# Other DMA rings for gates, rows and v tiles, and a new engine order, at the start of an attention and feed-forward kernel

## Chip, cores, metric

One core of one Trainium2 chip. The metric is device microseconds of one execution; lower is better. Times are medians of the executions of one kernel. Engines: PE is TensorE (PEld its weight loads), ACT is ScalarE, DVE is VectorE, POOL is GpSimd, SP is SyncE, which here only issues DMA; a "q" behind a name (SPq, ACTq, POOLq) marks its DMA issues. Every execution has a mean granted TensorE clock beside its time, 1.00 being full speed.

## The reference

```python
# q, k, v: (8 batches, 8 heads, 576, 64); f: (8, 8, 576) in 0.8 .. 1.0
scores = matmul(q, k^T) / 8
cum    = cumsum(log(clip(f, 1e-4, 1)), axis=-1)
scores = where(causal, -1e9, scores + cum[..., :, None] - cum[..., None, :])
x      = softmax(scores) @ v                  # heads put side by side: 4608 tokens x 512
out    = (silu(x @ w_gate) * (x @ w_val)) @ w_out     # 512 -> 1536 -> 512
```

## The kernel before

Everything runs in bf16 on PE. The decay enters the scores as extra rows of the operands: four bf16 rows (8 cum, and -8 cum in three parts `hi`, `mid`, `lo`) are computed on 64 partitions and put by DMA under q and k, on partitions 64 to 67 of `QK`. So no score can start before its rows have landed. The second half of a sequence needs the second half of the rows.

A planner in Python gives every operation an engine, the operations it waits for, a priority (`key`) and an earliest time (`ready`), simulates the engines, and emits the instructions in the order so found.

The parts that matter here:

```python
def ld_f(e, c):                     # gates, two halves of a sequence
    E[e].dma_start(out=lf[:, CUTS[c]], in_=f.rearrange("b h s -> (b h) s")[:, CUTS[c]])
o_f   = [op(("ACT", 0.5), ld_f, c, key=-20, ...) for c in range(2)]
o_dec = [op(("DVE", 0.25), fill, dec[r][:, 0 if r else 1], 1.0, key=-17) for r in range(4)]
# ... clip, Ln, scan, hi, mid, lo of each half ...

def row(e, r, c):                   # one decay row (4 in a set) into QK, on SyncE
    E[e].dma_start(out=QK[D + r : D + r + 1, p0:p1, :, x]..., in_=dec[r][2 * p0 : 2 * p1, :, x])

def blank(e, what):                 # GpSimd memsets of QK's tails, of VB's pads ...
    nc.gpsimd.memset(QK[:, :, 1::2, S:], 0.0) ...

def ld_v(e, b, n, bv):              # v tile n of batch b: 128 rows (the last: 64) x 8 heads, float32
    m = min(P, S - n * P)
    nc.sync.dma_start(out=natv[bv.i][:m], in_=v[b, :, n * P : n * P + m].rearrange("h p d -> p h d"))

def cast_v(e, b, n, bv):            # to bf16, for batch 0 on GpSimd
    copy(e, VB[hvb[b].i][:m, n, :, :D], natv[bv.i][:m])

def mask(e, h, i):                  # causal mask of the exponentials, on GpSimd
    nc.gpsimd.affine_select(out=d, in_=d, ...)

W_AT = [-2.8, -18.4, -0.5, 15.6]; CHAIN = 30.6; KEY_Q = -17.9      # (cut: priorities that a search tuned)
V0_KEY = (-1.0, -3.2, 17.1, 22.4, 21.2)                            # v tiles 0..4 of batch 0
```

The first batch goes through attention in two parts: its first 256 queries (`PTa`) and the rest (`PT`, called the second part below). For each part: scores on PE, exponentials on ScalarE, masks on GpSimd, products with v on PE. The weights `wg` and `wv` of the feed-forward stream in meanwhile on GpSimd's DMA queue, with a conversion to bf16.

The softmax here doesn't subtract the row's maximum and nothing guards it: scores larger than these inputs give would overflow.

Of the kernel before, what the change touches and what calls it, by code (L numbers as in the profile page):

```python
# [9 lines left out]
F32 = mybir.dt.float32  # L10
BF16 = mybir.dt.bfloat16
AF = mybir.ActivationFunctionType
ALU = mybir.AluOpType
# [20 lines left out]
class Plan:  # L34
# [32 lines left out]
    def run(self, idle=None):  # L67
# [6 lines left out]
        busy = {e: 0.0 for e in engines}  # L74
        ready = {e: [] for e in engines}
        lanes = [0.0] * 8
        rings, moved = {"HW": [], "POOL": []}, 0.0
        nlane, left, t, seq = 0, len(self.ops), 0.0, 0
        events = []

        def share(busy):
            if rings["POOL"] and rings["POOL"][0][1] is None:
                return [1.0 if r is rings["POOL"] else 0.1 for r in busy]
            return [0.6, 0.65] if len(busy) > 1 else [1.0]

        def push(at, kind, o):
            nonlocal seq
# [6 lines left out]
        while left:  # L94
# [4 lines left out]
            while events and events[0][0] <= t + 1e-9:  # L99
                _, _, kind, o = heapq.heappop(events)  # L100
                if kind in ("queue", "dma"):
                    busy_rings = [r for r in rings.values() if r]
                    for r, x in zip(busy_rings, share(busy_rings)):
                        r[0][0] -= (t - moved) * x
                        while r and r[0][0] < 1e-6:
                            over, n = r.pop(0)
                            if r:
                                r[0][0] += over
                            if n is None:
                                continue  # L110
                            n.done = t + 1.0
                            push(n.done, "end", n)
                            push(n.done + n.late, "done", (n, None, False))
                    moved = t
                    if kind == "queue":
                        r = rings["POOL" if o.ran == "POOL" else "HW"]
                        if o.ran == "POOL" and not r:
                            r.append([1.5, None])
                        r.append([o.dma, o])
                    busy_rings = [r for r in rings.values() if r]  # L120
                    if busy_rings:
                        push(t + min(r[0][0] / x for r, x in zip(busy_rings, share(busy_rings))), "dma", None)
                elif kind == "ready":
                    for e in o.eng:
                        ready[e].append(o)
                elif kind == "end":
                    if o.dma is not None and o.lane is not None:
                        lanes[o.lane] = t
                    for b in o.use:
                        b.left -= 1  # L130
                        if not b.left:
                            self.free[b.pool].append(b.i)
                    left -= 1
                elif kind == "done":
                    o, e, own = o
                    for s in o.next:
                        if (list(s.eng) == [e]) != own:
                            continue
                        s.wait -= 1
                        if not s.wait:  # L140
                            push(max(t, s.ready), "ready", s)
# [61 lines left out]
def kernel(ctx, tc, q, k, v, f, w_gate, w_val, w_out, out):  # L203
# [5 lines left out]
    P = 128  # L209
# [113 lines left out]

    def scan(e, c):
        x = CUTS[c]
        nc.vector.tensor_tensor_scan(out=cum[:, x], data0=lf[:, x], data1=zero[:, x], op0=ALU.add, op1=ALU.add,
                                     initial=cum[:, HALF - 1 : HALF] if c else 0.0)

    def scaled(e, dst, src, x):
# [11 lines left out]
    def fill(e, dst, x):  # L341
        E[e].memset(dst, x)

    o_f = [op(("ACT", 0.5), ld_f, c, key=-20, dma=(0.3, 0.35)[c]) for c in range(2)]
    o_one = op(("DVE", 0.1), fill, warm, 1.0, key=-20)
    o_wln = op(("ACT", 1.5), lambda e: nc.scalar.activation(warm, warm, AF.Ln), after=[o_one], key=-18)
    o_id = op(("POOL", 0.8), lambda e: make_identity(nc, ident[:, :]), key=KEY_Q + 3.5)
    o_zero = op(("DVE", 0.55), fill, zero, 0.0, key=-18)
    o_dec = [op(("DVE", 0.25), fill, dec[r][:, 0 if r else 1], 1.0, key=-17) for r in range(4)]
    ROWS0 = ((0, FB, CUTS[0]), (0, FB, CUTS[1]), (FB, FIRST * FB, slice(0, S)))  # L350

    def row(e, r, c):
# [7 lines left out]
    for c in range(2):  # L360
        x, kc, d = CUTS[c], (-50, CHAIN)[c], (256, 320)[c] / 960
        o = op(("DVE", 0.15 + d), clip, c, after=[o_f[c]], key=-51)
        o = op(("ACT", 0.2 + d), log, c, after=[o, o_wln], key=-51)
        o_ln = o
        o_cum = op(("DVE", 0.15 + 1.9 * d), scan, c, after=[o, o_zero, o_cum], key=kc)
        o_hi = op(("DVE", 0.2 + 0.6 * d), scaled, dec[1][:, 1, x], cum[:, x], -8.0, after=[o_cum], key=kc)
        o_up = op({"ACT": 0.2 + d, "POOL": 0.3 + d}, scaled, dec[0][:, 0, x], cum[:, x], 8.0, after=[o_cum], key=kc)
        o_r1 = op(("DVE", 0.15 + d), rest, x, after=[o_hi], key=kc)
        o_mid = op(("DVE", 0.15 + 0.6 * d), scaled, dec[2][:, 1, x], r1[:, x], 1.0, after=[o_r1], key=kc)
        o_lo = op(("DVE", 0.15 + d), lowest, x, after=[o_mid], key=kc)  # L370
        o_chain += [o_up, o_hi, o_mid, o_lo]
        for n in ((0,), (1, 2))[c]:
            o_row.append([op((ROWQ[c], 0.75), row, r, n, after=[o_dec[r]] + o_chain[r::4], key=ROW_KEY[n] + r, dma=(0.1, 0.1, 0.2)[n],
                             ready=(0, 0, ROW_AT)[n] + 0.8 * r) for r in range(4)])

    def blank(e, what):
# [8 lines left out]
        else:  # L385
            nc.gpsimd.memset(VB[what][:, :, :, D:], 1.0)
            nc.gpsimd.memset(VB[what][LAST:, NB - 1], 0.0)

    o_vb = [op(("POOL", 0.8), blank, 0, key=-15), op(("POOL", 0.8), blank, 1, key=2020, ready=24.0),
            op(("POOL", 0.8), blank, 2, key=4020, ready=40.0)]  # L390
    o_qkz = op(("POOL", 0.9), blank, "qk", key=-14)
    o_pt = op(("POOL", 1.4), blank, "pt", key=310, ready=10.0)
    o_edge = op(("SP", SPi), blank, "edge", after=[o_qkz], key=900, dma=0.2, ready=30)
    o_warm = op(("ACT", 1.4), lambda e: nc.scalar.activation(warm, lf[:1, :1], AF.Exp), after=[o_ln], key=-51)
# [45 lines left out]

    def ld_v(e, b, n, bv):
        m = min(P, S - n * P)
        nc.sync.dma_start(out=natv[bv.i][:m], in_=v[b, :, n * P : n * P + m].rearrange("h p d -> p h d"))

    def cast_v(e, b, n, bv):
        m = min(P, S - n * P)
# [4 lines left out]

    def values(b, n, key, after=(), ready=0.0):
        bv = Buf("nv")
        o = op(("SP", SPi), ld_v, b, n, bv, take=[bv], key=key, dma=1.2 if n < NB - 1 else 0.6, after=after,
               ready=ready, late=LATE if b >= FIRST else LATE0, tag=("ldv", b, n))
        eng = copier(H * D, False) if b == 1 else ("POOL", pool(H * D))
        v_ready[b, n] = op(
            eng, cast_v, b, n, bv, after=[o, o_vb[b % NVB]], use=[bv], key=key, tag=("castv", b, n),
            **({"take": [hvb[b]]} if n == 0 else {}),
        )  # L460
        if n:
            v_ready[b, n].use.append(hvb[b])
            hvb[b].left += 1
            v_ready[b, n].after.append(v_ready[b, 0])
# [5 lines left out]
    def queries(p, key, after=(), ready=0.0):  # L470
        done = []
        b = p // FB
        if b < PEB:
            rest = []
            for x, nm in enumerate("qk"):
                bn, bt = Buf("natw" if b == 1 else "nat"), Buf("t", ("f", BORROW), ("s", 22.0))
                kk = key + 2 * x
                o1 = op(("POOL", 0.35), ld_qk, p, nm, bn, take=[bn], key=kk, dma=0.74,
                        ready=max(ready, release(p) - SLACK) + 0.3 * x, tag=("ldqk", p), late=(0.0, LATE0, LATE)[b])
                o3 = op(("PE", mm(*[QP] * QT)), turn, bn, bt, after=[o1, o_id], take=[bt], use=[bn], key=kk, tag=("turn", p))  # L480
                if b == 1:
                    wo_free.append(o3)
                for a in range(2):
                    first = not rest and not a
                    rest.append(op(
                        {"ACT": 0.75, "DVE": 0.8}, straighten, p, x, a, bt, after=[o3] + ([rest[0]] if rest else []),
                        take=[hqk[p]] if first else [], use=[bt] if first else [bt, hqk[p]], key=kk, tag=("str", p),
                    ))
# [275 lines left out]
    return plan, span  # L764


W_AT = [-2.8, -18.4, -0.5, 15.6]
WO_AT = [28.1, 28.3, 50.7, 57.5]
Q1_AT = [24.1, 27.1, 27.5, 39.5]
V1_AT = 28.1  # L770
CHAIN = 30.6
DEC_AT = 38.0
V0_KEY = (-1.0, -3.2, 17.1, 22.4, 21.2)
V0_AT = (4.8, 3.2, 1.8, 10.5, 7.7)
NARROW_AT = 72.0
FREE = 87.7
LATE = 2.0
ROWS = ("SP", 0.45)
SLACK = 24.0
IDLE_TO = 40.0  # L780
BORROW = 33.9
KEY_Q = -17.9
ROWQ = ("SP", "SP")
ROW_KEY = (-17.7, 22.4, 64.6)
ROW_AT = 28.1
LATE0 = 1.0
# [1 line left out]
_INS = ['q', 'k', 'v', 'f', 'moe_w_gate', 'moe_w_val', 'moe_w_out']  # L788
_OUTS = [((4608, 512), 'float32')]
# [25 lines left out]
```

## Time and profile before

| | value |
|---|---|
| time, median of 3 | 407.28 us (406.62 to 407.53) |
| profile: span, PE busy, mean granted clock | 404.9 us, 96%, 0.978 |
| first score / first exponential of the second part | 14.52 / 27.39 us |
| first product of the second part / first gate matmul | 30.19 / 36.73 us |

From 40 us on PE is full, so only the start is open. The first view is the chain of waits of the kernel before, in order of time (start, length, what; PE, DVE and POOL entries are work, DMA entries transfers, SPq issues):

```profile
1.39 5.33 DMA xT<-in_f_dram
...
13.45 0.38 DVE xT L339
13.83 0.73 SPq L354
...
14.65 10.52 DMA QK<-xT
...
25.31 1.55 PE ps L528 x8
```

The decay arithmetic ends at 13.8 us, its last row is issued at once, and then 10.5 us pass before the rows have landed and PE can score the second part. The timeline of the same stretch (start, length, engine, line, operation, tiles, count; in brackets the idle time before, and its releaser) shows what stands on SyncE's ring between the rows, and what follows:

```profile
10.05 0.73 SPq L443 DMA_DIRECT2D natv<-in_v_dram  x1
10.89 1.50 SPq L354 DMA_DIRECT2D QK<-xT  x2
12.44 0.63 SPq L443 DMA_DIRECT2D natv<-in_v_dram  x1
13.16 2.90 SPq L354 DMA_DIRECT2D QK<-xT  x3
...
25.24 0.61 POOL L302 CAST VB<-natv 128x512 bf16<-128x512 f32 x1 [4.67 <-DMA natv<-in_v_dram]
25.31 1.55 PE L528 MATMUL ps<-QK 68*128 68x192 bf16 x8 [4.51 <-DMA QK<-xT]
27.39 3.73 ACT L536 ACTIVATE PT<-ps 128x512 bf16<-128x512 f32 x9
28.33 0.73 POOL L545 TENSOR_SCALAR_AFFINE_SELECT PT<-PT 128x128 bf16<-128x128 bf16 x3
30.19 0.70 PE L559 MATMUL ps<-VB,PT 128*128 128x65 bf16 x9
```

The DMA queues from 18 to 25 us (packets, MB, share of 16 engines' time):

```profile
q0 software_dynamic: 1314, 0.98, 89.8%
q1 hardware_dynamic: 1314, 0.35, 36.9%
```

q0 is the weights' queue, q1 SyncE's ring: equal counts, but 0.98 MB against 0.35 MB: 1282 of q0's packets have 768 bytes, 1220 of q1's have 256. A v tile of 128 rows x 8 heads is 1024 packets of 256 bytes; the row issued behind it landed at 25.17 us, 10.52 us after its issue.

Last, busy time in stretches of the kernel before (stretch: length, then busy time and count of PE, PEld, DVE, ACT, POOL; then granted clock, DMA share, GB/s):

```profile
11.25:14.66 3.41, 1.73 (x19) 1.18 (x18) 2.54 (x5) 1.83 (x3) 3.41 (x19) 1.00 1.22 181
14.66:18.07 3.41, 3.41 (x32) 2.98 (x31) 1.06 (x2) 2.77 (x5) 1.98 (x4) 0.50 1.28 193
20.00:25.00 5.00, 0.80 (x6) 0.50 (x4) 0.71 (x3) 0.10 (x1) 0.57 (x1) 0.50 1.28 193
25.00:30.00 5.00, 4.69 (x38) 3.60 (x39) 1.56 (x6) 3.37 (x9) 4.38 (x13) 0.50 1.28 195
100.00:200.00 100.00, 99.46 (x828) 55.90 (x826) 60.23 (x113) 58.33 (x121) 35.16 (x99) 1.00 0.77 146
```

PE is busy 0.80 of 5 us from 20 to 25 us and 99.5 of 100 us later. The clock fell to 0.50 at 14.66 us and came back at 31.73 us.

### The profile page before, as it was taken

The page shows a single profiled execution, that of the slowest core. Times are in us where ns is not written, and L with a number is a line of the kernel's source. Part 1 is how long each engine was busy: PE and PEld are TensorE (multiplying, and loading weights), DVE is VectorE, ACT ScalarE, POOL GpSimd, SP SyncE. Part 2 cuts the span into 40 slices and gives each one's busy share as a digit, 9 for nine tenths or more (in the row PEclk, how much of TensorE's full clock was granted, in tenths as well). Part 3 has the DMA queues.
Part 4 walks back from the last instruction along what each step waited for, and adds up shares of the span by engine and source line. Part 5 has one row for each costly group of instructions (what it writes and reads, how often), then busy time and mean ns, then how long its engine had stood idle before and what let it go on. Part 6 is the DMA issues. An engine that isn't in the chain of part 4 may idle for free.

```text
span 404.9 us, 8469 instructions
## 1 busy us (share of the span) xinstructions
PE 388.6 (96%) x3175; PEld 227.3 (56%) x3175; DVE 230.2 (57%) x444; ACT 220.9 (55%) x448; POOL 133.0 (33%) x369
## 2 busy tenths in 40 slices
PE   5859999999999999999999999999999999999996
PEld 4647778645555555555555655655565444444542
DVE  7625888527873477247733775177724861770850
ACT  5738787438764466456465654666666322322321
POOL 8848446803352144225142522542233000000000
PEclk9759999999999999999999999999999999999999
DMA  9999738647944985599579759955211002002002
GB/s 171 189 195 191 168 61 135 94 123 130 155 105 110 174 178 106 126 199 197 116 118 248 131 105 172 192 143 106 52 53 52 2 0 105 1 0 105 0 12 82
DMA packets 103897, 46.57 MB, mean 115 GB/s; under 512 B 87792, under 2 KB 98736, under 8 KB 103536
## 3 DMA queue, kind: packets, MB, share of 16 engines
q1 hardware_dynamic: 92400, 31.72, 37.9%
q0 software_dynamic: 11296, 14.16, 21.8%
q8 instruction: 25, 0.41, 0.4%
q10 hardware_dynamic: 160, 0.15, 0.1%
q14 instruction: 16, 0.13, 0.1%
HBM read 38.34 MB, written 15.78 MB: 134 GB/s over the span
## 4 chain that ended last, share of the span: by engine, by line
PE 85%; DVE 5%; DMA 4%; ACT 1%; issue 1%; POOL 1%; SPq 0%; ACTq 0%; DVEq 0%; POOLq 0%
PE ps L660 42%; PE ps L675 24%; PE ps L528 10%; PE ps L559 7%; DMA QK<-xT 3%; DVE QK L302 2%; PE ps L583 2%; DMA xT<-in_f_dram 1%; DVE hh L671 1%; DVE th L668 1%; POOL wo L410 1%; ACT PT L536 1%; PE ps L416 1%; POOL PT L545 0%; DVE xT L333 0%
## 5 line engine op out<-in xcount | busy, mean ns | idle before, releaser
L660 PE MATMUL ps<-xT,wv 128*128 128x512 bf16 (+3 forms) x480 | 113.0, 357 | 0.0
L660 PE MATMUL ps<-xT,wg 128*128 128x512 bf16 (+3 forms) x480 | 113.0, 357 | 0.0
L668 DVE SCALAR_TENSOR_TENSOR th<-th,ps 128x512 f32<-128x512 f32 (+3 forms) x120 | 75.6, 630 | 55.2 <-ACT th L664 54.9
L675 PE MATMUL ps<-wo,hh 128*128 128x512 bf16 (+1 forms) x444 | 106.5, 379 | 0.0
L664 ACT ACTIVATE th<-ps 128x512 f32<-128x512 f32 (+3 forms) x120 | 66.5, 555 | 69.4 <-PE ps L660 68.1
L536 ACT ACTIVATE PT<-ps 128x512 bf16<-128x512 f32 (+2 forms) x192 | 91.9, 511 | 22.2 <-PE ps L528 13.1
L671 DVE TENSOR_TENSOR hh<-th,ps 128x512 bf16<-128x512 f32 (+3 forms) x120 | 76.1, 635 | 13.2 <-PE ps L660 1.1
L528 PE MATMUL ps<-QK 68*128 68x320 bf16 (+4 forms) x448 | 76.6, 270 | 6.7 <-DMA QK<-xT 5.9
L545 POOL TENSOR_SCALAR_AFFINE_SELECT PT<-PT 128x128 bf16<-128x128 bf16 (+1 forms) x192 | 52.1, 274 | 78.5 <-ACT PT L536 72.5
L660 PEld LDWEIGHTS <-wg 128*128 128x128 bf16 x480 | 44.6, 97 | 36.5 <-issue 0.7
L660 PEld LDWEIGHTS <-wv 128*128 128x128 bf16 x480 | 45.0, 97 | 35.7 <-issue 0.7
L675 PEld LDWEIGHTS <-hh 128*128 128x128 bf16 (+1 forms) x444 | 41.6, 98 | 39.5 <-issue 0.8
L545 POOL TENSOR_SCALAR_AFFINE_SELECT PTa<-PTa 128x256 bf16<-128x256 bf16 x64 | 25.8, 407 | 93.5 <-ACT PTa L536 92.2
L679 ACT ACTIVATE ot<-ps 128x512 f32<-128x512 f32 (+1 forms) x37 | 22.1, 597 | 56.9 <-PE ps L675 56.4
L559 PEld LDWEIGHTS <-PT 128*128 128x128 bf16 x768 | 40.4, 98 | 15.7 <-POOL PT L545 0.4
L559 PE MATMUL ps<-VB,PT 128*128 128x65 bf16 x768 | 48.2, 194 | 0.1
L528 PEld LDWEIGHTS <-QK 68*128 68x128 bf16 x448 | 35.8, 100 | 20.4 <-issue 5.6
L566 DVE RECIPROCAL rc<-ps 128x5 f32<-128x5 f32 (+2 forms) x64 | 12.3, 193 | 54.0 <-PE ps L559 53.8
L536 ACT ACTIVATE PTa<-ps 128x384 bf16<-128x384 f32 x64 | 30.8, 488 | 22.1 <-PE ps L528 22.0
L573 DVE TENSOR_TENSOR xn<-ps,rc 128x320 bf16<-128x320 f32 x56 | 27.5, 492 | 1.9
L302 DVE COPY QK<-ps 64x576 bf16<-64x576 bf16 x24 | 18.7, 797 | 14.1 <-PE ps L416 13.3
L302 DVE COPY xT<-ps 128x576 bf16<-128x576 bf16 (+2 forms) x34 | 14.5, 427 | 20.3 <-PE ps L583 20.3
(47 smaller groups left out, 192.7 us busy)
## 6 DMA issues: line engine op xcount, KB each, us to landing
out_dram<-ot SPq DMA_DIRECT2D x35, 256.0 KB
natv<-in_v_dram SPq DMA_DIRECT2D x32, 256.0 KB
qk_d<-in_q_dram POOLq DMA_DIRECT2D x5, 576.0 KB, 6.9
qk_d<-in_k_dram POOLq DMA_DIRECT2D x5, 576.0 KB, 7.8
wg<-in_moe_w_gate_dram POOLq DMA_DIRECT2D x4, 384.0 KB, 13.4
wv<-in_moe_w_val_dram POOLq DMA_DIRECT2D x4, 384.0 KB, 12.9
wo<-in_moe_w_out_dram POOLq DMA_DIRECT2D x4, 384.0 KB, 5.8
QK<-qk_d SPq DMA_TRANSPOSE x80
```

The costliest lines, as they stand in the source:

```text
L302: E[e].tensor_copy(dst, src)
L528: nc.tensor.matmul(s[:, c : c + w], QK[:KR, hqk[p].i, 2 * j + 1, kt * P : (kt + 1) * P], QK[:KR, hqk[p].i, 2 * j, q0 : q0 + w], start=True ...
L536: nc.scalar.activation(place(h, i)[:, OFFS[i] : OFFS[i] + c], ps(bs)[:, :c], AF.Exp, scale=0.125)
L545: nc.gpsimd.affine_select(out=d, in_=d, pattern=pat, compare_op=ALU.is_ge, fill=0.0, base=0, channel_multiplier=-1,)
L559: nc.tensor.matmul(o[:, lo : lo + D + 1], pt[:, c : c + P], VB[hvb[b].i][:, kt, hb, : D + 1], start=first and n == 0, stop=last and n == l ...
L573: nc.vector.tensor_mul(XN[bx.i][:, qb : qb + nq, j], o, r)
L660: nc.tensor.matmul(ps(bf)[:, :n], w[:, ko, fc * P : (fc + 1) * P], xT[:, ko, t0 : t0 + n], start=(ko == 0), stop=(ko == KD - 1))
L664: nc.scalar.activation(TH[bt.i][:, :n], ps(bf)[:, :n], AF.Tanh, scale=0.5)
L668: nc.vector.scalar_tensor_tensor(out=t, in0=t, scalar=1.0, in1=ps(bf)[:, :n], op0=ALU.add, op1=ALU.mult)
L671: nc.vector.tensor_mul(HH[:, bh.i, lo : lo + n], TH[bt.i][:, :n], ps(bf)[:, :n])
L675: nc.tensor.matmul(ps(bf)[:m, :DM], HH[:, hs[fc].i, lo : lo + m], wo[:, fc, :], start=(fc == 0), stop=(fc == KF - 1))
L679: nc.scalar.activation(OT[bo.i][:m], ps(bf)[:m, :DM], AF.Copy, scale=0.5)
```

## The change

Its intent: let the decay rows land earlier by giving SyncE's ring to gates and rows, and moving the first three v tiles of batch 0 to ScalarE's ring (tile 3 goes early on SyncE, tile 4, of 64 rows, late on SyncE); issue the loads of q and k before GpSimd's memsets; make VectorE's fills shorter by writing two bf16 ones as one float; and let the planner model three rings instead of two, whose shares follow the size of their packets (a model; equal counts of packets, as above, give such shares), with all priorities searched anew.

```diff
-    o_f = [op(("ACT", 0.5), ld_f, c, key=-20, dma=(0.3, 0.35)[c]) for c in range(2)]
+    o_f = [op(("SP", 0.5), ld_f, c, key=-70, dma=(0.3, 0.35)[c], pk=50) for c in range(2)]
...
-    o_zero = op(("DVE", 0.55), fill, zero, 0.0, key=-18)
-    o_dec = [op(("DVE", 0.25), fill, dec[r][:, 0 if r else 1], 1.0, key=-17) for r in range(4)]
+    o_zero = op(("DVE", 0.1), fill, zero[:, :1], 0.0, key=-60)
+    o_dec = [op(("DVE", 0.36), fill, dec[r][:, 0 if r else 1].bitcast(F32), 1.0 + 2.0**-9 - 2.0**-16, key=-52) for r in range(4)]
...
-    o_vb = [op(("POOL", 0.8), blank, 0, key=-15), ...
-    o_qkz = op(("POOL", 0.9), blank, "qk", key=-14)
+    o_vb = [op(("POOL", 0.8), blank, 0, key=KEY_Q + 17), ...
+    o_qkz = op(("POOL", 0.9), blank, "qk", key=KEY_Q + 18)
...
     def ld_v(e, b, n, bv):
-        nc.sync.dma_start(out=natv[bv.i][:m], in_=v[b, :, n * P : n * P + m]...)
+        E[e].dma_start(out=natv[bv.i][:m], in_=v[b, :, n * P : n * P + m]...)
...
-        o = op(("SP", SPi), ld_v, b, n, bv, ...
+        o = op((V0_ENG[n] if b == 0 else "SP", SPi), ld_v, b, n, bv, ..., pk=22, ...
...
-W_AT = [-2.8, -18.4, -0.5, 15.6]
+W_AT = [6.8, -9.5, 10.4, 20.2]
-V0_KEY = (-1.0, -3.2, 17.1, 22.4, 21.2)
-V0_AT = (4.8, 3.2, 1.8, 10.5, 7.7)
+V0_KEY = (-18.9, -18.8, -14.4, 16.0, -20)
+V0_AT = (-0.3, -11.7, 6.9, -18.8, 15.6)
+V0_ENG = ("ACT", "ACT", "ACT", "SP", "SP")
... (cut: the planner's model of the rings; a dozen other priorities)
```

More of the change, by code (lines that the diff above doesn't have):

```diff
@@ L76, in run @@
         lanes = [0.0] * 8
-        rings, moved = {"HW": [], "POOL": []}, 0.0
+        rings, moved = {"SP": [], "ACT": [], "POOL": []}, 0.0
         nlane, left, t, seq = 0, len(self.ops), 0.0, 0
@@ L82, in share @@
             if rings["POOL"] and rings["POOL"][0][1] is None:
-                return [1.0 if r is rings["POOL"] else 0.1 for r in busy]
-            return [0.6, 0.65] if len(busy) > 1 else [1.0]
+                return [1.0 if r is rings["POOL"] else 0.2 for r in busy]
+            x = sum(r[0][1].pk for r in busy)
+            return [(1.15 if len(busy) > 1 and rings["POOL"] else 1.0) * r[0][1].pk / x for r in busy]
         def push(at, kind, o):
@@ L115, in run @@
                     if kind == "queue":
-                        r = rings["POOL" if o.ran == "POOL" else "HW"]
+                        r = rings[o.ran]
                         if o.ran == "POOL" and not r:
@@ L325, in scan @@
         x = CUTS[c]
-        nc.vector.tensor_tensor_scan(out=cum[:, x], data0=lf[:, x], data1=zero[:, x], op0=ALU.add, op1=ALU.add,
+        nc.vector.tensor_tensor_scan(out=cum[:, x], data0=lf[:, x], data1=zero[:, :1].to_broadcast([BH, x.stop - x.start]), op0=ALU.add, op1=ALU.add,
                                      initial=cum[:, HALF - 1 : HALF] if c else 0.0)
@@ L342, in fill @@
         E[e].memset(dst, x)
-    o_f = [op(("ACT", 0.5), ld_f, c, key=-20, dma=(0.3, 0.35)[c]) for c in range(2)]
-    o_one = op(("DVE", 0.1), fill, warm, 1.0, key=-20)
+    o_f = [op(("SP", 0.5), ld_f, c, key=-70, dma=(0.3, 0.35)[c], pk=50) for c in range(2)]
+    o_one = op(("DVE", 0.1), fill, warm, 1.0, key=-61)
     o_wln = op(("ACT", 1.5), lambda e: nc.scalar.activation(warm, warm, AF.Ln), after=[o_one], key=-18)
     o_id = op(("POOL", 0.8), lambda e: make_identity(nc, ident[:, :]), key=KEY_Q + 3.5)
-    o_zero = op(("DVE", 0.55), fill, zero, 0.0, key=-18)
-    o_dec = [op(("DVE", 0.25), fill, dec[r][:, 0 if r else 1], 1.0, key=-17) for r in range(4)]
+    o_zero = op(("DVE", 0.1), fill, zero[:, :1], 0.0, key=-60)
+    o_dec = [op(("DVE", 0.36), fill, dec[r][:, 0 if r else 1].bitcast(F32), 1.0 + 2.0**-9 - 2.0**-16, key=-52) for r in range(4)]
     ROWS0 = ((0, FB, CUTS[0]), (0, FB, CUTS[1]), (FB, FIRST * FB, slice(0, S)))
@@ L372 @@
         for n in ((0,), (1, 2))[c]:
-            o_row.append([op((ROWQ[c], 0.75), row, r, n, after=[o_dec[r]] + o_chain[r::4], key=ROW_KEY[n] + r, dma=(0.1, 0.1, 0.2)[n],
+            o_row.append([op((ROWQ[c], 0.75), row, r, n, after=[o_dec[r]] + o_chain[r::4], key=ROW_KEY[n] + r, dma=(0.1, 0.1, 0.2)[n], pk=34,
                              ready=(0, 0, ROW_AT)[n] + 0.8 * r) for r in range(4)])
@@ L387, in blank @@
             nc.gpsimd.memset(VB[what][LAST:, NB - 1], 0.0)
-    o_vb = [op(("POOL", 0.8), blank, 0, key=-15), op(("POOL", 0.8), blank, 1, key=2020, ready=24.0),
+    o_vb = [op(("POOL", 0.8), blank, 0, key=KEY_Q + 17), op(("POOL", 0.8), blank, 1, key=2020, ready=24.0),
             op(("POOL", 0.8), blank, 2, key=4020, ready=40.0)]
-    o_qkz = op(("POOL", 0.9), blank, "qk", key=-14)
+    o_qkz = op(("POOL", 0.9), blank, "qk", key=KEY_Q + 18)
     o_pt = op(("POOL", 1.4), blank, "pt", key=310, ready=10.0)
@@ L442, in ld_v @@
         m = min(P, S - n * P)
-        nc.sync.dma_start(out=natv[bv.i][:m], in_=v[b, :, n * P : n * P + m].rearrange("h p d -> p h d"))
+        E[e].dma_start(out=natv[bv.i][:m], in_=v[b, :, n * P : n * P + m].rearrange("h p d -> p h d"))
     def cast_v(e, b, n, bv):
@@ L453, in values @@
         bv = Buf("nv")
-        o = op(("SP", SPi), ld_v, b, n, bv, take=[bv], key=key, dma=1.2 if n < NB - 1 else 0.6, after=after,
+        o = op((V0_ENG[n] if b == 0 else "SP", SPi), ld_v, b, n, bv, take=[bv], key=key, dma=1.2 if n < NB - 1 else 0.6, pk=22, after=after,
                ready=ready, late=LATE if b >= FIRST else LATE0, tag=("ldv", b, n))
@@ L477, in queries @@
                 kk = key + 2 * x
-                o1 = op(("POOL", 0.35), ld_qk, p, nm, bn, take=[bn], key=kk, dma=0.74,
+                o1 = op(("POOL", 0.64), ld_qk, p, nm, bn, take=[bn], key=kk, dma=0.74,
                         ready=max(ready, release(p) - SLACK) + 0.3 * x, tag=("ldqk", p), late=(0.0, LATE0, LATE)[b])
@@ L764 @@
     return plan, span
-W_AT = [-2.8, -18.4, -0.5, 15.6]
-WO_AT = [28.1, 28.3, 50.7, 57.5]
-Q1_AT = [24.1, 27.1, 27.5, 39.5]
-V1_AT = 28.1
-CHAIN = 30.6
-DEC_AT = 38.0
-V0_KEY = (-1.0, -3.2, 17.1, 22.4, 21.2)
-V0_AT = (4.8, 3.2, 1.8, 10.5, 7.7)
+W_AT = [6.8, -9.5, 10.4, 20.2]
+WO_AT = [38.8, 38.2, 36.6, 51.1]
+Q1_AT = [19.5, 27.1, 34.3, 41.4]
+V1_AT = 24.4
+CHAIN = 32.3
+DEC_AT = 50.7
+V0_KEY = (-18.9, -18.8, -14.4, 16.0, -20)
+V0_AT = (-0.3, -11.7, 6.9, -18.8, 15.6)
 NARROW_AT = 72.0
-FREE = 87.7
+FREE = 53.2
 LATE = 2.0
@@ L780 @@
 IDLE_TO = 40.0
-BORROW = 33.9
-KEY_Q = -17.9
+BORROW = 34.7
+KEY_Q = -31.3
 ROWQ = ("SP", "SP")
-ROW_KEY = (-17.7, 22.4, 64.6)
-ROW_AT = 28.1
+ROW_KEY = (-20, 13.3, 49.0)
+ROW_AT = -16.2
 LATE0 = 1.0
+V0_ENG = ("ACT", "ACT", "ACT", "SP", "SP")
 _INS = ['q', 'k', 'v', 'f', 'moe_w_gate', 'moe_w_val', 'moe_w_out']
```

## The prediction

The sum came to 4 us: rows landing near 21.5 us for 25.2, exponentials of the second part at 22 to 24 us for 27.4, 403.3 us in total for 407.2. The 270 ns of a shorter fill are the author's estimate, about half of the measured 538. For the dummies, the kernel before shows 0.13 us each at full clock (eight in 1.04 us from 9.60 us) and 0.27 at half (four in 1.06 us from 18.77 us).

> **What bounds it now.** From 40 us on TensorE: the busy times by stretch give PE 99.5 of 100 us from 100 to 200, 100 of 100 from 200 to 300. Only the start is open: the chain of waits reads: the gates' second load (1.39 us, 5.33 us long), decay arithmetic on VectorE among copies of q, k (to 13.8 us), then a 10.5 us wait for the DMA that puts decay rows into QK (14.65 to 25.17); PE resumes at 25.31, ScalarE's exponentials of the second part at 27.4. From 20 to 25 us PE is busy 0.80 of 5 us. The granted clock was 0.50 from about 15 to 31 us.
>
> **Why the rows are late.** In the timeline the rows of the second half are issued at 10.9 to 15.4 us on SyncE, behind two v tiles (10.05, 12.44) of the same ring. From 18 to 25 us the DMA queues moved 1314 packets of GpSimd's weight stream and 1314 of SyncE's: one for one, weight packets of 768 bytes against v packets of 256. So a v tile of 1024 packets crawls, and the rows behind it. [...]
>
> **What changes.**
> - The rows get SyncE's ring with only the gates and one early v tile ahead; three v tiles go to ScalarE's ring. The rows' wait should shrink from 10.5 to about 4.5 us, as for the first rows (issue 9.33 us, scores 14.52).
> - But VectorE's order now clips both halves before the first scan and puts seven copies of q, k (0.8 us each) ahead of the last part of the second half's chain: it ends near 17 us instead of 13.8. Rows land near 21.5 us instead of 25.2.
> - VectorE's five fills of 538 ns become four of about 270 and a tiny one. Worth little: they ended at 4.0 us, when the gates' first half landed (first clip 4.11).
> - GpSimd's memsets (0.74 and 0.95 us) move behind q, k, which are issued up to 1.7 us earlier. Weights start about 2 us later.
> - PE's order holds 73 dummy matmuls for 59; after the first score 29 for 11. At the cold clock they took 0.27 us each: 18 more are 5 us, an estimate. [...] If PE stays warm the dummies are cheap; if cold, they eat the gain.
> - ScalarE's order has all eight first-part exponentials before the second part, which cannot start before about 21 us: the gain is at most about 7 us.
>
> All of this is critical until the second part starts; then PE is full, so the gain should reach the end.
>
> **Prediction.** Second-part exponentials start at 22 to 24 us rather than 27.4; 4 us gained, 403.3 us in total, 8 times in 10 between 399.8 and 407.2. Chances: over 2% faster 0.10, within 2% 0.87, slower 0.03.
>
> **Right if:** the chain shows the rows' wait at 4 to 5 us; PE idle from 20 to 25 us gone; PE from 100 us unchanged, shifted by about 4 us; fills in no wait; first scores within 1 us of 14.
>
> **Wrong if:** the clock stays at 0.50 through 30 us and 29 dummies run at 0.27 us (no gain); the rows still land after 24 us because three rings share the engines; v casts on GpSimd, now behind six weight issues, hold the first products; or later q, k loads of batch 1 delay the first gates (new waits at 35 to 45 us).

## The result, and the profile after

In the first measurement the changed kernel took 405.85 us (median of 404.93, 405.55, 406.15 and one odd execution of 1433.5 us, which the ratio leaves out) against 407.21 us for the kernel before: ratio 0.9961, 95% interval 0.9937 to 0.9984. Measured again, as the first experiment below: 405.14 against 407.49 us, ratio 0.9933 (0.9911 to 0.9955). Ratios are the mean time of one kernel's fast executions over that of the other's in the same rounds, so not quite the ratio of the medians. Between the medians of the fast executions (405.55 us in the first measurement) the gain is 1.7 and 2.4 us, not 4.

The profile of the first measurement fell in the odd execution, in which a 512-column matmul took 820 ns (216 ns in the kernel before, from start to start) while the profile gives the clock as 1.00; it explains nothing about the change. All lines "after" are therefore from the repeat, the same kernel. (Its profiled execution was the slowest of that repeat: 405.95 us, span 404.0 us, clock 0.992.)

The chain of waits of the changed kernel:

```profile
10.34 4.54 DMA QK<-xT
...
18.41 0.68 SPq L356
...
19.14 9.34 DMA natv<-in_v_dram
...
28.53 0.61 POOL VB L303
29.14 0.60 POOL wo L412
29.73 0.32 POOL PT L547
...
30.10 0.46 PE ps L561 x5
```

The rows' long wait is gone from the chain: the first rows cost 4.54 us. In its place stands the last v tile of batch 0: issued on SyncE at 19.14 us, landed 9.34 us later, cast on GpSimd, and only then the first mask and the first product of the second part. The timeline of the changed kernel says the same with the idle times:

```profile
19.14 0.71 SPq L445 DMA_DIRECT2D natv<-in_v_dram  x1
...
23.90 6.12 ACT L538 ACTIVATE PT<-ps 128x512 bf16<-128x512 f32 x15 [2.39 <-PE ps L530]
...
28.53 0.61 POOL L303 CAST VB<-natv 64x512 bf16<-64x512 f32 x1 [3.55 <-DMA natv<-in_v_dram]
29.73 2.82 POOL L547 TENSOR_SCALAR_AFFINE_SELECT PT<-PT 128x128 bf16<-128x128 bf16 x12
30.10 0.46 PE L561 MATMUL ps<-VB,PT 128*128 128x65 bf16 x5 [1.57 <-POOL PT L547]
```

The exponentials of the second part start 3.5 us earlier than before (23.90 for 27.39), as forecast. GpSimd then idles 3.55 us for the tile, with the masks behind it in its list, and the first product starts at 30.10 us, where before it was 30.19. A lead of 3.5 us on ScalarE became one of 0.1 us on PE within six microseconds.

| milestone, us | before | changed (repeat) | lead |
|---|---|---|---|
| first score | 14.52 | 14.97 | -0.4 |
| first exponential of the second part | 27.39 | 23.90 | +3.5 |
| first mask of the second part | 28.33 | 29.73 | -1.4 |
| first product of the second part | 30.19 | 30.10 | +0.1 |
| first gate matmul | 36.73 | 36.13 | +0.6 |
| end of the profile | 404.9 | 404.0 | +0.9 |

The DMA queues of the changed kernel from 19 to 29 us, the time of that tile:

```profile
q0 software_dynamic: 1962, 1.46, 101.1%
q1 hardware_dynamic: 1011, 0.31, 34.3%
```

The tile has 512 packets of 256 bytes. It shared the time with 1962 weight packets, nearly two for each of the 1011 of SyncE's ring. The packet records say more. From 19 to 23 us (`prof again --dma --window 19:23`) SyncE's ring moved 48 packets and the weights' queue 1055; the first 256-byte packet after the tile's issue moved at 23.25 us, 4.1 us after it. So nearly half of the 9.34 us passed before anything of the tile moved; what held it there was not shown, and only in the rest did its packets move beside those of the weights. The kernel before had the same 4.1 us: its 64-row tile, issued at 10.05 us, sent its first packet at 14.17.

Busy time in stretches of the changed kernel:

```profile
20.00:25.00 5.00, 3.74 (x51) 3.22 (x50) 1.79 (x7) 2.61 (x7) 4.98 (x15) 1.00 1.30 199
25.00:30.00 5.00, 3.19 (x22) 1.44 (x20) 1.01 (x5) 5.00 (x13) 1.47 (x4) 0.99 1.41 152
26.45:29.86 3.41, 1.85 (x11) 0.71 (x9) 0.00 (x0) 3.41 (x9) 1.33 (x3) 1.00 1.46 128
29.86:33.27 3.41, 3.17 (x41) 2.69 (x42) 0.58 (x2) 2.40 (x6) 3.41 (x14) 0.50 1.28 193
100.00:200.00 100.00, 99.91 (x841) 56.48 (x840) 60.23 (x114) 59.37 (x121) 35.67 (x101) 1.00 0.80 144
```

PE's gap at 20 to 25 us is filled (3.74 of 5 us for 0.80), at full clock. But from 25 to 30 us PE is busy 3.19 of 5 us, where before it was 4.69. And just when the products come, at 29.86 us, the clock falls to 0.50 until 36.68 us. The stretch 26.45 to 29.86 us, with PE busy 1.85 of 3.41 us, precedes it.

### The profile page after: what moved, and what is told of

Read it like the earlier page. It is cut to its first block, busy times and chain, and to the rows that moved or that the text cites. A ratio compares the mean times of both kernels' runs of the same rounds, so it can differ in the third digit from the quotient of the medians.

```text
span 1431.7 us, 8507 instructions
## 1 busy us (share of the span) xinstructions
PE 1424.2 (99%) x3189; PEld 569.1 (40%) x3189; DVE 233.2 (16%) x447; ACT 237.5 (17%) x444; POOL 135.1 (9%) x370
## 4 chain that ended last, share of the span: by engine, by line
PE 99%; POOL 0%; issue 0%; ACT 0%; ACTq 0%; POOLq 0%
PE ps L662 49%; PE ps L677 25%; PE ps L530 11%; PE ps L561 7%; PE ps L585 2%; PE ps L763 2%; PE ps L418 2%; POOL xT L412 0%; ACT ot L681 0%; POOL ident masks.py:199 0%; POOL ident masks.py:197 0%; ACTq L681 0%; POOLq L802 0%
## 5 line engine op out<-in xcount | busy, mean ns | idle before, releaser
L662 PE MATMUL ps<-xT,wv 128*128 128x512 bf16 (+3 forms) x480 | 388.7, 1020 | 0.0
L662 PE MATMUL ps<-xT,wg 128*128 128x512 bf16 (+3 forms) x480 | 387.7, 1016 | 0.0
L677 PE MATMUL ps<-wo,hh 128*128 128x512 bf16 (+1 forms) x444 | 382.9, 1098 | 0.0
L530 PE MATMUL ps<-QK 68*128 68x320 bf16 (+4 forms) x448 | 210.2, 637 | 0.0
L662 PEld LDWEIGHTS <-wv 128*128 128x128 bf16 x480 | 104.5, 221 | 194.5 <-issue 193.1
L662 PEld LDWEIGHTS <-wg 128*128 128x128 bf16 x480 | 99.8, 212 | 199.1 <-issue 198.3
L677 PEld LDWEIGHTS <-hh 128*128 128x128 bf16 (+1 forms) x444 | 94.1, 216 | 206.4 <-issue 204.9
L561 PEld LDWEIGHTS <-PT 128*128 128x128 bf16 x768 | 106.7, 186 | 77.4 <-issue 65.8
L561 PE MATMUL ps<-VB,PT 128*128 128x65 bf16 x768 | 120.0, 350 | 0.0
L585 PE MATMUL ps<-ident,xn 128*128 128x128 bf16 x160 | 43.2, 493 | 0.0
```

The lines of the kernel that those rows point to most:

```text
L530: nc.tensor.matmul(s[:, c : c + w], QK[:KR, hqk[p].i, 2 * j + 1, kt * P : (kt + 1) * P], QK[:KR, hqk[p].i, 2 * j, q0 : q0 + w], start=True ...
L561: nc.tensor.matmul(o[:, lo : lo + D + 1], pt[:, c : c + P], VB[hvb[b].i][:, kt, hb, : D + 1], start=first and n == 0, stop=last and n == l ...
L585: nc.tensor.transpose(t[:, n * P : (n + 1) * P], XN[bx.i][:, qb + n].rearrange("p h d -> p (h d)"), ident)
L662: nc.tensor.matmul(ps(bf)[:, :n], w[:, ko, fc * P : (fc + 1) * P], xT[:, ko, t0 : t0 + n], start=(ko == 0), stop=(ko == KD - 1))
L677: nc.tensor.matmul(ps(bf)[:m, :DM], HH[:, hs[fc].i, lo : lo + m], wo[:, fc, :], start=(fc == 0), stop=(fc == KF - 1))
```

## The experiments

**Theory A:** the change does what it should for the rows, but GpSimd, waiting for the last v tile, holds the masks and with them the products; a tile that lands early gives back the forecast gain. **Rivals:** B, GpSimd's moved memsets or the order of weights cost the lead; C, the dummy matmuls or the half clock eat it; D, the rows were never worth 4 us.

### again: the changed kernel, once more

No edit.

> The changed kernel unaltered, for a profile of its usual state: its recorded profile fell in an execution of 1433.5 us in which every 512-column matmul took about 820 ns. Expected: 405 to 406 us, ratio to before 0.994 to 0.998. Theory A (the start did gain about 4 us and something after it gave 2.5 us back): second-part exponentials start at 22 to 24 us, and new waits show between 30 and 100 us. Theory B (the start itself gained little): second-part exponentials start at 25 us or later, because rows or v tiles still land late or dummy matmuls fill PE.

Measured: 405.14 us (404.31 to 405.95), 407.49 before, ratio 0.9933 (0.9911 to 0.9955), clocks of the four executions 0.992 to 0.995. The 1433-us execution did not come back, and the gain remains well below 1%.

### v4_act and v4_sp: the last v tile of the changed kernel, issued early

One load moves. In v4_act it follows tile 2 on ScalarE's ring (7.56 us), in v4_sp it follows tile 3 on SyncE's (2.69 us), where 19.14 us was.

```diff
     def ld_v(e, b, n, bv):
+        if (b, n) == (0, NB - 1):
+            return                                    # (cut: an assertion on the buffer)
         E[e].dma_start(out=natv[bv.i][:m], in_=v[b, :, n * P : n * P + m]...)
+        if (b, n) == (0, NB - 2):                     # v4_act: (0, 2)
+            E[e].dma_start(out=natv[NB - 1][:LAST], in_=v[b, :, (NB - 1) * P : S]...)
```

> As v4_act, but issued on SyncE right after its own first v tile (about 2.7 us), before any row. Theory A: the same gain as v4_act, less up to 0.6 us because 512 more small packets run beside the q, k loads and ahead of the first rows. Rival B: no change from the changed kernel, or slower by the 0.6 us.

The 0.6 us in it are the author's estimate; no run measures them alone.

v4_sp measured 403.51 us (402.76 to 403.65) against 407.08, ratio 0.9909 (0.9893 to 0.9925): 3.6 us, the gain that had been forecast for the change. Its timeline:

```profile
25.62 0.64 POOL L303 CAST VB<-natv 64x512 bf16<-64x512 f32 x1
...
26.82 3.11 POOL L552 TENSOR_SCALAR_AFFINE_SELECT PT<-PT 128x128 bf16<-128x128 bf16 x12
...
29.13 0.32 PE L566 MATMUL ps<-VB,PT 128*128 128x65 bf16 x5
```

The cast of the last tile has no bracket: it waited for nothing. The masks start at 26.82 us (29.73 before this edit) although the exponentials start later than in the changed kernel (24.65 for 23.90). The first product gains only 1.0 us. The rest comes after it, at full clock (it was never below full from 13.8 to 399.5 us), and the stretch that in the changed kernel had PE busy 1.85 of 3.41 us reads here, in the busy times by stretch,

```profile
27.45:30.87 3.42, 3.19 (x42) 1.98 (x41) 0.13 (x1) 3.42 (x10) 3.24 (x12) 1.00 1.30 203
```

One load moved, no other instruction changed, and the forecast gain is there in all four executions: the slowest of them (403.65 us) is faster than the fastest of the seven fast executions of the changed kernel (404.31 to 406.15). It speaks against D. But two other runs with the tile early, v4_act here and v4_sp_memsets below, do not repeat it on the median.

> The changed kernel, but the last tile of v of batch 0 (64 rows) is issued from ScalarE right after the tile before it (about 7 us) instead of from SyncE behind the second rows (19.14 us); nothing else in any engine's order changes. Theory A (the lead of 3.5 us at the second-part exponentials was given back because GpSimd waits for this tile, 24.9 to 28.5 us, and the masks stand behind it): that wait disappears, the first second-part mask moves from 29.73 us to 25 to 26 us, the clock stays at 1.0 past 30 us, time 402 to 403.5 us, ratio to before 0.986 to 0.990. Rival B (the lead would have been lost anyway, to ScalarE, VectorE or the q, k loads of batch 1 before the first gates): the wait disappears, first gate at 36 us as before, time unchanged within 0.5 us.

v4_act measured 405.31 us (403.21 to 406.3) against 407.08, ratio 0.994 (0.9903 to 0.9978): on the median no gain over the changed kernel. Its profile shows the tile's wait gone too, the first mask at 28.39 us, and a lead of 2.1 us over the changed kernel's trace as late as the 200th gate matmul (174.85 for 176.98 us). Then it lost it, in the chain of waits:

```profile
206.34 5.23 DMA QK<-dec_d
```

A DMA of decay rows of a later batch was issued late by SyncE and held PE for 2.5 us. So the profiled execution (406.24 us) gained its tile and lost it again to another wait. Whether the unprofiled ones, of which one took 403.21 us, did the same is not known; this run is a miss for the plain form of theory A, "any early place will do".

### before_split: the kernel before, with only its last two v tiles on ScalarE's ring

```diff
-        nc.sync.dma_start(out=natv[bv.i][:m], ...)
+        q = nc.scalar if b == 0 and n >= 3 else nc.sync
+        q.dma_start(out=natv[bv.i][:m], ...)
```

> The kernel before with one edit: v tiles 3 and 4 of batch 0 are issued from ScalarE instead of SyncE, at the same places of the plan, so the decay rows no longer stand behind them in SyncE's ring. Theory A (the rows were late because of the ring alone): second rows land at 18 to 20 us instead of 25.2, PE resumes its scores by 21 us, time 402.5 to 405 us (ratio 0.988 to 0.995). Rival C (the rows were late because all rings share saturated DMA engines): rows still land after 23 us, time within 1 us of before.

Measured: 405.52 us (404.63 to 406.43), ratio 0.9962 (0.9941 to 0.9984). This does the core of the change alone: nothing stands between the rows any more. Its timeline:

```profile
21.48 2.19 ACT L537 ACTIVATE PT<-ps 128x512 bf16<-128x512 f32 x5
...
25.41 0.61 POOL L302 CAST VB<-natv 128x512 bf16<-128x512 f32 x1 [5.13 <-DMA natv<-in_v_dram]
...
28.50 2.12 POOL L546 TENSOR_SCALAR_AFFINE_SELECT PT<-PT 128x128 bf16<-128x128 bf16 x9
...
29.47 0.70 PE L560 MATMUL ps<-VB,PT 128*128 128x65 bf16 x9
```

The second part's exponentials start 5.9 us earlier than before, and the cast of the v tile 0.17 us later: 25.41 us, with a wait of 5.13 us. The tile was issued on ScalarE's ring at 10.36 us and landed at 25.35; from 18 to 25 us that ring moved 880 packets, SyncE's 925 and the weights' queue 1212. First mask and first product stay near 28.5 and 29.5 us. So the other ring let the rows pass but did not bring the tile sooner. The two waits of the kernel before thus ended together, and ending the rows' alone is worth 1.6 us, where ending both, in the next two runs, is worth 5.5 and 5.7.

### before_vfirst and before_vact: end both waits

Both are the kernel before with its last two v tiles ahead of the weight stream, whose first load is issued at 8.78 us: on SyncE behind the first three (2.79 us on), or on ScalarE's ring right after ScalarE's exponential-table load (6.81 and 7.50 us).

```diff
 # before_vact
+    def exp_table(e):
+        nc.scalar.activation(warm, lf[:1, :1], AF.Exp)
+        for n2, i2 in ((4, 3), (3, 4)):            # (cut: m2, the rows of the tile)
+            nc.scalar.dma_start(out=natv[i2][:m2], in_=v[0, :, n2 * P : n2 * P + m2]...)
-    o_warm = op(("ACT", 1.4), lambda e: nc.scalar.activation(warm, lf[:1, :1], AF.Exp), ...)
+    o_warm = op(("ACT", 1.4), exp_table, ...)
     def ld_v(e, b, n, bv):
+        if b == 0 and n >= 3:
+            return
 # before_vfirst: the same two loads, from SyncE, right behind the third v tile
```

> The kernel before with one edit: the last two v tiles of batch 0 are issued from SyncE directly after the first three (by about 4 us), ahead of all rows, rather than at 10.05 and 12.44 us. Theory F (two waits ended together in the kernel before, rows on PE at 25.17 us and the v tile on GpSimd at 25.24 us, both because small packets crawl beside the weights; only removing both helps): second rows land by 20 us, GpSimd's wait for v vanishes, masks of the second part start by 24 us, time 402 to 404 us (ratio 0.988 to 0.993), where the split of rings alone gave 0.996. Rival G (the start of the kernel before has a third limit near 25 us): time within 1 us of before.

before_vfirst measured 402.05 us (401.54 to 402.15) against 407.54, ratio 0.9865 (0.9852 to 0.9877). Second-part exponentials 22.05, first mask 23.23, first product 24.81 us; its profile ends 4.6 us before that of the kernel before (span 400.3 us). It did so although its clock was at 0.50 from 22.37 to 29.20 us, just as its second part began.

> The kernel before with the last two v tiles issued from ScalarE right after its second table load (about 8 us), so neither ahead of the rows in SyncE's ring nor ahead of q, k, but still before the weight stream starts near 13 us. If what matters is only that these tiles precede the weight stream: 402 to 403 us like the edit that put them first on SyncE (402.05). If they do not finish before the weights: v lands after 17 us and the gain is smaller, 403 to 405 us.

before_vact measured **401.52 us** (400.63 to 402.81) against 407.21, ratio 0.9854 (0.9833 to 0.9875). It has the best median, faster than both the one before and the changed one; its interval overlaps that of before_vfirst. Its timeline, with the cast of the last v tile, which no wait precedes:

```profile
20.25 0.62 POOL L302 CAST VB<-natv 128x512 bf16<-128x512 f32 x1
...
21.86 9.03 ACT L545 ACTIVATE PT<-ps 128x512 bf16<-128x512 f32 x22
...
23.36 2.59 POOL L554 TENSOR_SCALAR_AFFINE_SELECT PT<-PT 128x128 bf16<-128x128 bf16 x9
24.10 0.43 PE L568 MATMUL ps<-VB,PT 128*128 128x65 bf16 x9
```

Both ends move: rows (exponentials at 21.86 us) and tiles (landed at 13.08 and 15.64 us), and the first product comes 6.1 us earlier than before. This small edit gains 1.5%, with none of the change's other parts.

### memsets_first and long_fills: undo the other parts of the change

memsets_first puts GpSimd's memsets of VB and QK back among the first q and k loads; long_fills puts VectorE's long fills back.

```diff
 # memsets_first (cut: blank leaves these two alone elsewhere)
-    o_id = op(("POOL", 0.8), lambda e: make_identity(nc, ident[:, :]), ...)
+    o_id = op(("POOL", 0.8), lambda e: (blank(e, 0, True), make_identity(nc, ident[:, :]), blank(e, "qk", True)), ...)
 # long_fills
+        E[e].memset(zero, 0.0)                   # all of it, where one column was filled
+        E[e].memset(dec[r][:, 0 if r else 1], 1.0)   # by bf16, where pairs were filled
```

> The changed kernel with GpSimd's first memsets (VB and QK) back around the identity, ahead of the second q load, as in the kernel before. In the changed kernel the copies of q, k wait for the QK memset at 10.7 us (1.33 us on ScalarE, 0.93 us on VectorE) and PE idles 1.88 us, so moving the fills behind the loads may have gained nothing. If the move helped: slower than the changed kernel by 0.5 to 1.7 us. If it only moved the wait: same within 0.5 us.

memsets_first: 403.65 us (403.12 to 405.18) against 407.08, ratio 0.9922 (0.9899 to 0.9946). Undoing this part costs nothing; it may help (three of its four executions are faster than all seven of the changed kernel), but its interval overlaps that of the changed kernel. The first mask is as late as in the changed kernel, 30.27 us, and yet its profile ends 2.2 us earlier (span 401.8 us). Between the first product and the first gate matmul pass 3.7 us (30.63 to 34.28), where the changed kernel took 6.0. What its trace has different there is the clock:

```profile
25.54:28.95 3.41, 3.26 (x29) 1.85 (x28) 1.62 (x6) 3.41 (x10) 1.51 (x2) 1.00 1.39 131
28.95:32.37 3.42, 2.30 (x44) 1.70 (x42) 0.23 (x2) 3.42 (x10) 3.31 (x12) 1.00 1.33 208
```

> The changed kernel with VectorE's fills as before: 64x576 zeros and four 64x576 bf16 fills, about 540 ns each, instead of one element and four of 288 float pairs. VectorE's fills would end near 3.8 us, and the first clip waits for the gates until 4.67 us. Theory: no change in the time within the noise of 0.3%. Rival: up to 1.3 us slower, the time that the fills grew.

long_fills: 405.03 us (403.95 to 406.37) against 407.54, ratio 0.9939 (0.9922 to 0.9956), as the changed kernel: the fills make no difference. Its stretches, cut where its clock changes:

```profile
27.91:31.32 3.41, 1.96 (x23) 0.98 (x22) 0.00 (x0) 3.23 (x9) 2.26 (x7) 1.00 1.42 132
31.32:34.73 3.41, 3.41 (x43) 2.91 (x42) 1.08 (x3) 2.50 (x6) 3.40 (x12) 0.50 1.27 192
```

Read together, three traces with nearly the same late first mask (29.73, 30.27 and 30.27 us) ran at half clock after it for 6.8 us (changed kernel), 3.4 us (long_fills) and not at all (memsets_first), and their profiles ended 0.9, 1.9 and 3.1 us before that of the kernel before (unrounded ends). The stretch before the fall has PE busy 1.85 us (changed) and 1.96 us (long_fills) of 3.41 us; one of 2.30 us (memsets_first) was not followed by a fall. This gives no threshold, though. Cut at the clock's own changes, the stretches before the twelve falls that the kept traces show before the end of the work have PE busy between 1.18 us (memsets_first, from 11.91 us) and 3.06 us (warm30, from 25.84 us), while stretches of 1.61 us (before_vact, from 11.75 us) and 1.87 us (v4_sp_memsets, from 14.10 us) were followed by none. PE's busy time as the profile records it does not tell which stretch brings half clock.

### warm30 and warm26: keep PE busy through the tile's wait

Both add dummy matmuls (256 columns, results never used) to the changed kernel: warm30 14 of them at the second part's first products, warm26 15 spread over the scores of the second part.

```diff
 # warm30, in the products' loop
+        if (h, i) == (0, 1):
+            for _ in range(14):
+                nc.tensor.matmul(o[:, :HALF], ident, ident.unsqueeze(1).to_broadcast([P, 2, P]), start=True, stop=True)
 # warm26: 9 single ones behind scores of heads 2 and up, 6 before the first of the second part's products
```

> The changed kernel with 14 more dummy matmuls on PE, put just before the first products of the second part, where PE waited 1.57 us for GpSimd's mask (28.5 to 30.1 us). Theory D (part of the loss is the clock: the wait for the late v tile left PE idle from 26 to 29.6 us, the throttle then granted 0.50 from 29.86 to 36.68 us, and that slowed the catching up): the clock stays at 1.0 past 30 us, first gates 1 to 2 us earlier than 36.1, time about 403.5 us (1.5 to 2 us under the changed kernel's 405.1). Rival E (only GpSimd's wait counts, PE's speed between 30 and 37 us is hidden): time unchanged within 0.5 us, even if the clock stays up.

warm30: 405.99 us (405.24 to 406.23), ratio 0.9961 (0.9949 to 0.9973). Inconclusive: the dummies stood behind the idle time, ran at half clock themselves (throttled 29.25 to 32.66 us) and pushed the first product to 32.50 us. It tests nothing.

> The changed kernel with 15 more dummy matmuls on PE: one after each of nine second-part scores from about 25 us on, and six just before the first second-part products, so that PE is busy from 25 us to 30 us while it waits for ScalarE and for GpSimd's late mask. The earlier 14 dummies in one place did not keep the clock up, so they did not test it. Theory D (about 2 of the 3 us that were lost come from the throttled window 29.86 to 36.68 us; three traces with the same late masks and 6.8, 3.4 and 0 us throttled after 29 us ended 0.9, 1.9 and 3.1 us under the kernel before): no throttled window between 29 and 37 us in most executions, time 403 to 404 us, ratio 0.990 to 0.992. Rival E (the clock is not what cost): throttle gone and time still 405.

warm26: 404.8 us (403.02 to 405.59, six executions) against 407.21, ratio 0.9926 (0.9901 to 0.995). In its profile PE was busy 3.34 of 3.42 us from 25.68 us and the clock stayed full from 22.27 us on; with the first mask at 29.32 us it ended 1.6 us before the changed kernel's. The timed median is only 0.3 us better, and its executions scatter: two near 403.1, the profiled one at 404.41, three near 405.5. So it supports the clock's part in the profiled execution and not in the median; nor do its executions follow the clock (403.19 us at 0.991, 405.18 us at 0.996).

### v4_sp_memsets and vfirst_fills: put parts together

v4_sp_memsets joins the edits of v4_sp and memsets_first. vfirst_fills is before_vfirst with the change's other idea, the memsets of QK and VB moved behind the second and fourth loads of k.

```diff
 # vfirst_fills, in the load of q and k
+        if (p, nm) == (1, "k"):
+            blank("POOL", "qk", True)
+        if (p, nm) == (3, "k"):
+            blank("POOL", 0, True)
```

> The changed kernel with both edits that gained alone: last v tile early on SyncE, GpSimd's memsets back ahead of the second q load. If they act on different waits: 401.5 to 402.5 us. If both only removed the same idle time at 26 to 30 us (and with it the throttled window): no faster than v4_sp alone, 403 to 404 us.

v4_sp_memsets: 404.22 us (402.73 to 405.82), ratio 0.9932 (0.9914 to 0.995): no sum of the two. Its six executions differ with the clock: 402.73 us at 0.999, 405.82 us at 0.983 (those of long_fills do not: 403.95 us at 0.987, 405.37 at 0.995). Its profiled execution, the fastest, has the early tile's gain: first mask at 27.19 us, end 3.2 us before the changed kernel's. But its ratio is that of the changed kernel (0.9933), so this is a second miss for theory A on the median, after v4_act.

> The kernel before with the last two v tiles first on SyncE, and GpSimd's memsets moved behind loads: the QK memset after the second pair of q, k, the VB memset after the last. In the v-first kernel PE waits 1.7 us for the second q, issued at 5.03 us. If that wait is on the path: 401.0 to 401.7 us. If the rows (issue 15.53 us, landing 20.5) set the start of the second part anyway: same as without it, 402 us within 0.4.

vfirst_fills: 403.34 us (401.76 to 404.86) against 407.21, ratio 0.99 (0.9875 to 0.9924), slower than before_vfirst with 0.9865. Moving the memsets behind the loads is not a gain of its own. Rival B is not settled: this run and memsets_first hint that the move costs something over 1 us, v4_sp_memsets against v4_sp (0.9932 for 0.9909) points the other way, and the order of the weights was not tested. What can be said is that the move brought no gain.

## Why the prediction was right or wrong

**Right: where the open time was.** Only the start changed. From 100 to 200 us PE was busy 99.91 of 100 us (99.46 before), and the fills are in no wait that matters (long_fills).

**Right: the rows' wait.** Forecast 4 to 5 us for 10.5, measured 4.94 us for the last row that PE waited for (issued at 18.41 us) and 4.54 us for the first rows; second-part exponentials forecast at 22 to 24 us, measured 23.90. The decay arithmetic ended at 18.38 us (forecast near 17), the rows landed at 23.35 us (21.5).

**Right: the dummies are cheap while the clock is full.** It was, to 29.86 us; eleven of them took 1.36 us together, from 20.46 us. The forecast had this as its main risk, and it did not happen at that place.

**Right about packets, as far as they were counted.** The forecast started from 1314 packets against 1314 in the kernel before; how the engines choose between queues was not shown. In before_split a v tile on a third ring came no sooner (10.36 to 25.35 us): the other ring changed who waits behind whom, and the tile still moved beside the weights (880 packets against 1212 from 18 to 25 us). before_vact uses ScalarE's ring as well, but issues the same 128-row tile 2.9 us earlier, at 7.50 us; it landed 8.1 us after its issue, where before_split's took 15.0.

**Wrong, the step that failed:** "All of this is critical until the second part starts; then PE is full, so the gain should reach the end." The second part did start 3.5 us earlier. But a second wait, GpSimd's for the last v tile, had been ending within 0.07 us of the first in the kernel before (4.67 us of idle, on an engine that the chain did not name). It was not shortened: the change issues that tile at 19.14 us, and it was cast at 28.53 us. The masks stood behind it in GpSimd's list (the first at 29.73 us), and the first product stayed at 30.10 us. The trace shows this wait directly, and v4_sp supports it as the cause of the lost gain: with that one load issued at 2.69 us the kernel takes 403.51 us, and the forecast was 403.3. before_split shows the same from the other side, and more clearly: rows alone, 0.9962; rows and tiles, 0.9865 (before_vfirst) and 0.9854 (before_vact). Not shown is that an early tile is enough in the changed kernel: v4_act and v4_sp_memsets lost the tile's wait in their profiles too, and their executions scatter from 402.73 to 406.3 us, while memsets_first, with the tile still late, came to 403.65 us.

The prediction had named the risk, "v casts on GpSimd, now behind six weight issues, hold the first products", but looked at GpSimd's issue time and not at the landing of the tile. The tile's place behind eight rows on SyncE was to be read from the emitted order, and the last of those rows could not be issued before the decay arithmetic ended, forecast near 17 us. In the kernel before, the same 64-row tile, issued at 10.05 us, had landed at 18.48. Those 8.4 us after 17 us, an estimate, put the landing past 25 us, later than the forecast exponentials; it was issued at 19.14 us and took 9.34.

**Also not foreseen: half clock after the wait.** The stretch from 26.45 to 29.86 us, with PE busy 1.85 us, was followed by 6.8 us at half clock. The throttled stretches named above are multiples of 3.41 us (17.07 in the kernel before, 6.82 in the changed kernel, 3.41 in long_fills). PE's busy time did not separate stretches of 3.41 us before a fall (1.18 to 3.06 us) from others (1.61 us and more). Nor did a full stretch bring the clock back at once: in the kernel before, the first one at half clock had PE busy 3.41 of 3.41 us (14.66 to 18.07), in the changed kernel 3.17 (29.86 to 33.27), and both were followed by another at 0.50. What decides was not shown. An estimate from the three traces above: of 3.1 us that separate memsets_first from the kernel before, the changed kernel's trace may have lost 2.2 to the clock. This is an observation across traces of kernels that differ in more than the clock. Against it stands before_vfirst, whose profile ended only 0.8 us after that of before_vact, with 6.8 us at half clock in its start where before_vact had none; the only run meant to test it that did keep the clock up, warm26, moved its profile by 1.6 us and its median by 0.3. What share of the loss is clock in the median execution stays open.

Also open: the late decay rows near 206 us in v4_act, in executions without a profile; why executions of one kernel with the early tile differ by 3 us; what passes in the 4.1 us between a tile's issue and its first packet; the 1433.5-us execution, seen once in 4 + 4 executions of the same kernel; and why DMA traffic slumps around 27 to 29 us (54 to 123 GB/s in the changed kernel, where the slices from 19 to 27 us have 184 to 236).

## What to carry to other kernels

Where a profile shows a wait on the chain, look at every other engine that is waiting at the same time: if one of those waits ends within a few hundredths of a microsecond, as here, shortening the first is worth little until the second goes too (1.6 of 5.5 us). Look for a load that stands before other work in an engine's list, and try it ahead of the bulk stream: moving it to another ring did not bring it sooner (landed at 25.35 us in before_split, cast at 25.24 us in the kernel before), and issuing it earlier did (landed at 15.64 us in before_vact). Before a gain from one wait is forecast to the end, add to each load's planned issue time the time that a load of its size took in the profile before. Read the granted clock just behind a wait as well: in the changed kernel 6.8 us at half clock followed a stretch with PE busy 1.85 of 3.41 us, in memsets_first none followed one of 2.30; that such idle time costs twice was not shown.
